# Weight sums moved from the mixer into the attention, and one chunk of convolution taps moved to ScalarE and GpSimd

## Chip, cores and metric

The kernel runs on one core of a Trainium2 chip. The metric is device time in microseconds (us) of one execution. Engines in the profile: PE is TensorE (PEld its weight loads), DVE VectorE, ACT ScalarE, POOL GpSimd, SP the engine that issues most transfers.

## What is computed

Linear attention over 8 batches x 8 heads x 576 positions, a gated mixer with a causal convolution of 5 taps, and an FFT mixing step with layer norm and an MLP (512 to 2048 to 512).

```
phi(x): p = x @ w_phi; p -= max|p|; [exp(p), exp(-p)]
kv, z = phi(k)^T v, sum phi(k);   attn = phi(q) kv / (phi(q) z)
gate = sigmoid(sum_k conv_w[k] * x[s - 4 + k]);  x = (gate * (x @ w_val)) @ w_out
u = x + real(fft(fft(x, axis=seq), axis=feature))
un = layernorm(u);  out = u + relu(un @ w_ch1) @ w_ch2
```

The weights are 64-bit floats in memory; the kernel converts them itself. The MLP's matrix products use a scheme with 7 products of 2x2 blocks in place of 8, which needs sums of the four quarters of each weight block.

## The kernel before

**Attention.** 16 units (a pair of batches, a pair of heads) of 5 groups of positions make 80 steps, written out in a fixed order in `run_attention`: in each step every engine gets its share of several groups (projection `pj`, maximum L260, subtraction L263, exponentials, `kv`, `nm`, transposes). Each engine works in the order in which its instructions were written, and so does the SP queue.

**Conversions.** Between them run 21 generators `convert` (L116), started one after another about three steps apart, each advanced at steps 0, 3, 4, 5, 6 and 8 after its start: load the raw words (L121), split low words on ScalarE (L131), three VectorE instructions on 128x1024 words (L133, L134, and the add at L135, which the profile shows as L62, the helper's line, `mt<-mt,cv`), exponent on ScalarE (L137), sign on ScalarE and two GpSimd multiplications (L139 to L141), then `done`. 16 of the 21 are blocks of `w_ch1` and `w_ch2` (`conv_mlp`, L376): their `done` stores four quarters, 512 KB, in `s_scr` in DRAM. Tile `mt` has two buffers, so L133 of a piece waits for the store of the piece two before it.

**Mixer.** The last steps of the attention and the mixer are noted as operations with costs and due times (`note_*`); `place_ops` (L1137) orders them per engine; operations that list two engines ("vp") go to VectorE or GpSimd as the planner sees fit, and its model lets GpSimd and VectorE operations on SBUF operands exclude each other. Per batch: taps of four channel chunks (`note_taps`: ScalarE the first, VectorE the other four of each), sigmoid, products `val` with w_val, gate, products `ps` with w_out, the FFT products. 16 times `note_sums` (L382) loads four quarters from `s_scr` to tile `ws`, makes four sums on GpSimd and stores them. The layer norm of the first block (`ln_first`) is put in by `ln0`, so many steps after each batch (L1093). For the first batch, taps of chunk 0 are made in the attention's last four steps (`tap_steps`, L484).

**MLP.** `note_mlp` runs 5 blocks of positions; its weights come from `s_scr` (`note_weights`, L681), and are split in two parts each.

Of the kernel before, what the change touches and what calls it, by code (L numbers as in the profile page):

```python
# [30 lines left out]
def f32(ap):  # L31
    return ap.bitcast(F32)
# [33 lines left out]
def attention_moe_mixer_kernel(  # L66
# [48 lines left out]

    def convert(i, src, n, shape, halve, done):  # L116
        raw = P["xf"].tile([128, 1024, 2], I32, tag="xf", name="raw64")[:, 0:n]
# [22 lines left out]
        nc.gpsimd.tensor_tensor(out=w, in0=w, in1=f32(ex), op=ALU.mult)  # L140
        nc.gpsimd.tensor_tensor(out=w, in0=w, in1=sg, op=ALU.mult)  # L141
        yield
        done(w.rearrange("p (k f) -> p k f", k=shape[0]))
# [60 lines left out]
    stg = pool(early, "stg", 2, side=R)  # L204
    vraw_p = pool(early, "vraw", 2, side=R)
    ps_pj = pool(early, "ps_pj", 2, PSUM, side=R)
    ap1 = pool(att, "ap1", 1)
# [165 lines left out]
    def slices(i, j, q):  # L373
        return s_scr[i][j // (i + 1)][q, :, j % (i + 1)].rearrange("q p o f -> p q (o f)")

    def conv_mlp(n, j, i):  # L376
        def done(t):
            nc.sync.dma_start(out=slices(i, j, slice(0, 4)), in_=t.rearrange("p (q o) f -> p q (o f)", o=2))
        s = (w_ch1, w_ch2)[i][j].bitcast(I32).rearrange("o p (q f) -> o p q f", q=4)
        return convert(n, s, 1024, (8,), False, done)  # L380

    def note_sums(n):  # L382
        i, j = wsteps[n]
        t = later("ws")
        a21, a11, a12, a22 = (t[:, k] for k in range(4))
        k21, k11, k12, k22 = keys = [("ws", k) for k in range(4)]
        o_dma([(t, slices(i, j, slice(0, 4)))], [], keys, 512)
        o_tt("p", a22, a21, a22, ALU.add, 256, [k21, k22], [k22])
        o_tt("p", a21, a11, a21, ALU.subtract, 256, [k11, k21], [k21])
        o_tt("p", a11, a22, a11, ALU.subtract, 256, [k22, k11], [k11])  # L390
        o_tt("p", a12, a12, a11, ALU.subtract, 256, [k12, k11], [k12])
        o_dma([(slices(i, j, slice(4, 8)), t)], keys, [("s", i, j)], 512)

# [5 lines left out]
    def put_table(dst, src):  # L399
        r, n = src.shape  # L400
        t = stg.tile([128, 580], F32, tag="tab", name="tab")
        nc.sync.dma_start(out=t[0:r, 0:n], in_=src)
        yield
        hi_act(dst, t[0:r, 0:n])
        yield
# [13 lines left out]
    def open_mix():  # L419
        p = pool(gx, "g0", 1, side=R)  # L420
        ws = pool(vx, "ws", 1, side=R)
        psv = pool(vx, "psv", 1, PSUM, side=R)
# [4 lines left out]
        for i in range(2):  # L427
            late["pv", i] = psv.tile([128, NE + 2], F32, name=f"val{i}")
            late["gv", i] = P["g"].tile([128, NE], F32, tag="gv", name="gv")
            late["gs", i] = P["g"].tile([128, 2, NE], F32, tag="gs", name="gs")  # L430
        late["ws"] = ws.tile([128, 4, 256], F32, name="ws")
        late["pa"] = psa.tile([128, 2, 512], F32, name="acc")
# [30 lines left out]

    wsteps = [(i, j) for j in range(NJ) for i in range(2)]

    def load_x(b):
# [17 lines left out]
    def tap_steps():  # L484
        t, acc = late["xf", 0], late["sg", 0]
        act.activation(out=acc, in_=shifted(t, 0, 4), func=ACTF.Copy, scale=cw[:, 0, 4:5])
        for k in range(4):
            vec.scalar_tensor_tensor(
                out=acc, in0=shifted(t, 0, k), scalar=cw[:, 0, k:k + 1], in1=acc, op0=ALU.mult, op1=ALU.add
            )  # L490
            yield

# [11 lines left out]
    def note_taps(b, m):  # L504
# [3 lines left out]
        acc, k = (s, sk) if first else (later("pa")[:, :, 0:HS], "pa")  # L508
        if b or m:
            o_act(acc, shifted(t, m, 4), ACTF.Copy, 685, [xk], [k], scale=cw[:, m, 4:5])  # L510
# [170 lines left out]
    def note_weights(c, n, first=[]):  # L681
# [11 lines left out]
        src = s_scr[c][j][q].rearrange("p n k f -> p (n k f)")  # L693
        o_dma([(f32(l), src)], [("s", c, x) for x in ((j,), (2 * j, 2 * j + 1))[c] if q > 3] + first + (over(s) if c == 0 and n < RING[0] else []), [lk], (128, 256)[c])
        o_hi(h, f32(l), cols, [lk], [hk])
# [253 lines left out]
    def note_W(b, c):  # L949
# [4 lines left out]
        for a in range(2):  # L954
# [10 lines left out]
            if c == 2 and a == 0:  # L965
                r = later(("xr", b % 2))
                o_hi(r[0:1], p[0:1], NE, [k], [("xr", b % 2, 0)])
                o_lo("v", r[32:33], p[0:1], r[0:1], NE, [k, ("xr", b % 2, 0)], [("xr", b % 2, 1)])
            o_act(t[:, c, a], p, ACTF.Copy, NE, [k] + [("s",) + wsteps[-1]] * w, [("x2", w, c, a)])
        if c >= 2:  # L970
# [86 lines left out]
    def note_mix():  # L1057
        rings = [[(("ps", i), later(("ps", i))) for i in range(n)] for n in (4, 5)]
        nonlocal ring
        ring = cycle(rings[0])  # L1060
        sums = iter(range(len(wsteps)))
        SUMS = [(1, 0, 1, 0, 1)] * 5 + [(1, 0, 0, 0, 0), (0,) * 5]

        def add_sums(n):
            for i in range(n):
                k = next(sums, None)
                if k is not None:
                    in_place(note_sums, k)

        ln0 = chain(ln_first(0), ln_first(1))  # L1070
# [6 lines left out]
        for b in range(NB - 1):  # L1077
            note_x(b + 1)
            for i, c in enumerate((0, 2, 1, 3)):
                if i < 3:  # L1080
                    note_taps(b + 1, i)
                    note_V(b + 1, i)
                note_W(b, c)
                add_sums(SUMS[b][i])
            add_sums(SUMS[b][4])
            note_taps(b + 1, 3)
# [5 lines left out]
            note_SD(b)  # L1092
            for k in range((0, 2, 1, 2, 1, 0, 0)[b]):  # L1093
                in_place(next, ln0, None)
# [434 lines left out]
```

## Time and profile before

| what | us |
|---|---|
| median of 3 runs | 1338.03 (1337.85 to 1338.59) |
| profiled execution | 1339.93 |
| its span, first to last instruction | 1338.1 |
| TensorE busy | 1302.2 (97%) |
| VectorE busy | 1186.8 (89%) |
| ScalarE busy | 925.5 (69%) |
| GpSimd busy | 699.2 (52%) |

Busy time is the time in which an engine executes something; matmuls are pipelined, so a busy TensorE isn't one at its peak. The attention takes the span's first 311 us, the mixer up to about 640 us, the MLP the rest. Idle time counts where the engine is the one that the others wait for, so the profile is read stage by stage.

### The profile page before, as it was taken

Reading aid. Unit: us, or ns where it says so; the run is one execution under the profiler, and the core shown is the slowest. Engines: PE = TensorE matmul, PEld = TensorE weight load, DVE = VectorE, ACT = ScalarE, POOL = GpSimd, SP = SyncE. Lnnn points to the kernel's source line nnn. Section 1 sums busy time; section 2 is a strip of 40 time slices with the busy share of each in tenths; the row PEclk is TensorE's granted clock in tenths of the full one; section 3 lists DMA queues with packets and bytes.
Section 4 is the critical chain, followed back from the end, with each engine's and each line's share of the span. In section 5 each row is a group of like instructions: output and inputs, shape, how many; then the busy total and the mean of one; then the engine's idle time right before and its main releaser. Section 6 shows DMA issues by size and latency. Waiting matters only on the chain.

```text
span 1338.1 us, 30770 instructions
## 1 busy us (share of the span) xinstructions
PE 1302.2 (97%) x11952; PEld 1188.0 (89%) x11952; DVE 1186.8 (89%) x1900; ACT 925.5 (69%) x1874; POOL 699.2 (52%) x599
## 2 busy tenths in 40 slices
PE   8999999999899998999999999999999999999998
PEld 7888888888899998998888888888888888889997
DVE  7999999989898998979998998898889989888875
ACT  6888888866555546565877686777777676776662
POOL 1534343404467566536655774488457945583321
PEclk9999999999999999999999999999999999999999
DMA  7578878643344453334633463347333743345322
GB/s 273 172 264 275 277 260 289 209 180 118 116 150 147 134 161 111 124 121 155 219 104 102 155 220 108 98 135 240 108 102 103 231 144 103 107 142 182 106 86 88
DMA packets 151598, 214.63 MB, mean 160 GB/s; under 512 B 16790, under 2 KB 112278, under 8 KB 151452
## 3 DMA queue, kind: packets, MB, share of 16 engines
q1 hardware_dynamic: 146992, 203.05, 47.5%
q10 hardware_dynamic: 4460, 9.62, 1.9%
q8 instruction: 94, 1.54, 0.5%
q14 instruction: 52, 0.43, 0.1%
HBM read 165.63 MB, written 46.99 MB: 159 GB/s over the span
## 4 chain that ended last, share of the span: by engine, by line
PE 74%; DVE 18%; DMA 2%; ACT 2%; issue 2%; POOL 1%; SPq 0%; DVEq 0%; POOLq 0%; ACTq 0%
PE x L62 15%; PE cx L62 15%; PE cy L62 11%; PE ps L62 10%; PE y L62 8%; PE val L62 4%; PE z L62 4%; DVE y L263 3%; DVE m L260 3%; DVE acc L62 2%; PE kv L62 2%; PE pj L62 2%; PE nm L62 2%; DVE mt L62 2%; PE yt L313 1%
## 5 line engine op out<-in xcount | busy, mean ns | idle before, releaser
L62 POOL TENSOR_TENSOR r<-r 128x256 fp32r<-128x256 f32 (+1 forms) x301 | 292.6, 989 | 242.8 <-ACT r L62 228.7
L62 PE MATMUL x<-un,r 128*128 128x462 f32 (+1 forms) x960 | 221.7, 372 | 2.2 <-ACT c L62 1.4
L62 ACT ACTIVATE r<-r 128x256 fp32r<-128x256 f32 (+1 forms) x420 | 193.2, 486 | 42.0 <-DMA r<-s_scr 40.7
L62 PE MATMUL cx<-h,r 128*128 128x462 f32 (+1 forms) x960 | 213.9, 371 | 1.1 <-DVE acc L62 1.1
L62 PEld LDWEIGHTS x<-un,r 128*128 128x128 f32 x960 | 180.3, 188 | 23.9 <-DVE c L62 1.9
L62 PEld LDWEIGHTS cx<-h,r 128*128 128x128 f32 x960 | 180.3, 188 | 22.1 <-DVE acc L62 1.9
L62 PE MATMUL cy<-h,r 128*128 128x462 f32 (+1 forms) x720 | 160.2, 371 | 0.0
L62 PEld LDWEIGHTS cy<-h,r 128*128 128x128 f32 x720 | 135.4, 188 | 15.3
L62 PE MATMUL val<-xh,wv 128*128 128x290 f32 x768 | 116.5, 300 | 9.2 <-DVE gv L62 4.5
L62 PEld LDWEIGHTS val<-xh,wv 128*128 128x128 f32 x768 | 106.6, 189 | 13.1 <-DVE gv L62 6.2
L62 PE MATMUL y<-un,r 128*128 128x462 f32 (+1 forms) x480 | 113.6, 371 | 0.0
L62 DVE SCALAR_TENSOR_TENSOR acc<-xf,cw,acc 128x576 f32<-128x576 f32 x128 | 105.0, 824 | 8.2 <-ACT acc L62 7.6
L62 PE MATMUL ps<-ge,wo 128*128 128x290 f32 x768 | 108.1, 297 | 2.2 <-DVE fs L62 1.4
L62 PEld LDWEIGHTS ps<-ge,wo 128*128 128x128 f32 x768 | 104.7, 189 | 3.2 <-DVE fs L62 1.6
L140 POOL TENSOR_TENSOR mt<-mt,cv 128x1024 f32<-128x1024 f32 (+1 forms) x21 | 47.5, 2263 | 105.8 <-ACT cv L137 101.6
L62 PEld LDWEIGHTS y<-un,r 128*128 128x128 f32 x480 | 90.2, 188 | 10.3
L62 DVE TENSOR_TENSOR acc<-cx,acc 128x924 f32<-128x924 f32 (+1 forms) x80 | 88.8, 1110 | 11.7 <-PE cx L62 9.7
L260 DVE TENSOR_REDUCE m<-pj 128x8 f32<-128x1024 f32 (+1 forms) x80 | 88.6, 1108 | 9.3 <-PE pj L62 9.3
L62 PE MATMUL kv<-vraw,ke 128*64 128x66 f32 x2560 | 93.4, 225 | 1.2 <-DVE kvT L305 0.5
L62 PE MATMUL pj<-wp,kqraw 64*128 64x128 f32 x1152 | 87.9, 290 | 5.0 <-DMA kqraw<-in_k_dram 4.7
L62 PEld LDWEIGHTS kv<-vraw,ke 128*64 128x64 f32 x2560 | 81.7, 137 | 11.7 <-ACT ke L272 1.1
L62 ACT ACTIVATE h<-z 128x462 fp32r<-128x462 f32 (+1 forms) x120 | 66.4, 553 | 34.9 <-DVE z L62 31.1
(176 smaller groups left out, 2809.5 us busy)
## 6 DMA issues: line engine op xcount, KB each, us to landing
r<-s_scr SPq DMA_DIRECT2D x280, 128.0 KB, 2.2
r<-s_scr SPq DMA_DIRECT2D x140, 256.0 KB, 2.6
raw<-in_w_ch_dram SPq DMA_DIRECT2D x32, 512.0 KB, 5.9
vraw<-in_v_dram SPq DMA_DIRECT2D x16, 660.0 KB, 9.3
x_scr<-xT SPq DMA_DIRECT2D x32, 288.0 KB, 2.3
xf<-x_scr SPq DMA_DIRECT2D x8, 1152.0 KB, 6.5
u_scr<-u ACTq DMA_DIRECT2D x8, 1152.0 KB, 4.5
kqraw<-in_k_dram SPq DMA_DIRECT2D x15, 576.0 KB, 5.6
```

Source lines behind the costliest of these rows:

```text
L62: return lambda *a, **k: f(*(resolve(x) for x in a), **{n: resolve(x) for n, x in k.items()})
L140: nc.gpsimd.tensor_tensor(out=w, in0=w, in1=f32(ex), op=ALU.mult)
L260: nc.vector.tensor_reduce(out=m, in_=pv, axis=AX.X, op=ALU.max, apply_absolute_value=True)
L263: nc.vector.tensor_tensor(out=y, in0=pv, in1=m.unsqueeze(3).to_broadcast([128, 2, 2 * n, F]), op=ALU.subtract)
L313: nc.tensor.transpose(t[:, h, j, :], y[:, h, n + j, :], ident)
```

## The change

- `convert` gets a hook `also`, called right after the two GpSimd multiplications. For the 16 MLP pieces it makes the four sums on GpSimd from the quarters that are still in SBUF, into a tile `s` (pool `sums`, one buffer). `done` then makes two stores on the SP queue, of the quarters and of the sums.
- `note_sums` with its 16 loads, 64 sums and 16 stores in the mixer is gone, with tile `ws`, and the waits for the sums in `note_weights` and `note_W`.
- The tables are loaded through the same one-buffer pool (before: two buffers of `stg`).
- `tap_steps` also makes the taps of chunk 1 of the first batch: in each of four steps a scaled copy on ScalarE and an addition on GpSimd, after one more copy at the start. `note_taps(0, 1)` then only notes the sigmoid.
- The steps of `ln0` are spread (1, 1, 2, 1, 1, 0, 0) in place of (0, 2, 1, 2, 1, 0, 0).

```diff
--- before.py
+++ after.py
@@ -113,7 +113,7 @@
         mm(o, al, bh, start=False, stop=last)
 
 
-    def convert(i, src, n, shape, halve, done):
+    def convert(i, src, n, shape, halve, done, also=None):
         raw = P["xf"].tile([128, 1024, 2], I32, tag="xf", name="raw64")[:, 0:n]
         raw_k = raw.rearrange("p n t -> p (n t)").rearrange("p (k f) -> p k f", k=shape[0])
         if shape[0] == 8:
@@ -139,6 +139,8 @@
         nc.scalar.activation(out=sg, in_=hi32, func=ACTF.Sign)
         nc.gpsimd.tensor_tensor(out=w, in0=w, in1=f32(ex), op=ALU.mult)
         nc.gpsimd.tensor_tensor(out=w, in0=w, in1=sg, op=ALU.mult)
+        if also:
+            also(w.rearrange("p (k f) -> p k f", k=4))
         yield
         done(w.rearrange("p (k f) -> p k f", k=shape[0]))
         yield
@@ -203,6 +205,7 @@
     y_p = pool(early, "y", 2, side=R)
     stg = pool(early, "stg", 2, side=R)
     vraw_p = pool(early, "vraw", 2, side=R)
+    sums_p = pool(early, "sums", 1, side=R)
     ps_pj = pool(early, "ps_pj", 2, PSUM, side=R)
     ap1 = pool(att, "ap1", 1)
     qe_p = pool(att, "qe", 4)
@@ -374,22 +377,22 @@
         return s_scr[i][j // (i + 1)][q, :, j % (i + 1)].rearrange("q p o f -> p q (o f)")
 
     def conv_mlp(n, j, i):
-        def done(t):
-            nc.sync.dma_start(out=slices(i, j, slice(0, 4)), in_=t.rearrange("p (q o) f -> p q (o f)", o=2))
-        s = (w_ch1, w_ch2)[i][j].bitcast(I32).rearrange("o p (q f) -> o p q f", q=4)
-        return convert(n, s, 1024, (8,), False, done)
-
-    def note_sums(n):
-        i, j = wsteps[n]
-        t = later("ws")
-        a21, a11, a12, a22 = (t[:, k] for k in range(4))
-        k21, k11, k12, k22 = keys = [("ws", k) for k in range(4)]
-        o_dma([(t, slices(i, j, slice(0, 4)))], [], keys, 512)
-        o_tt("p", a22, a21, a22, ALU.add, 256, [k21, k22], [k22])
-        o_tt("p", a21, a11, a21, ALU.subtract, 256, [k11, k21], [k21])
-        o_tt("p", a11, a22, a11, ALU.subtract, 256, [k22, k11], [k11])
-        o_tt("p", a12, a12, a11, ALU.subtract, 256, [k12, k11], [k12])
-        o_dma([(slices(i, j, slice(4, 8)), t)], keys, [("s", i, j)], 512)
+        t = {}
+
+        def sums(w):
+            t["w"], t["s"] = w, sums_p.tile([128, 4, 256], F32, tag="s", name="s")
+            a21, a11, a12, a22 = (w[:, k] for k in range(4))
+            s21, s11, s12, s22 = (t["s"][:, k] for k in range(4))
+            nc.gpsimd.tensor_tensor(out=s22, in0=a21, in1=a22, op=ALU.add)
+            nc.gpsimd.tensor_tensor(out=s21, in0=a11, in1=a21, op=ALU.subtract)
+            nc.gpsimd.tensor_tensor(out=s11, in0=s22, in1=a11, op=ALU.subtract)
+            nc.gpsimd.tensor_tensor(out=s12, in0=a12, in1=s11, op=ALU.subtract)
+
+        def done(_):
+            for q, x in enumerate((t["w"], t["s"])):
+                nc.sync.dma_start(out=slices(i, j, slice(4 * q, 4 * q + 4)), in_=x)
+        src = (w_ch1, w_ch2)[i][j].bitcast(I32).rearrange("o p (q f) -> o p q f", q=4)
+        return convert(n, src, 1024, (8,), False, done, sums)
 
     def conv_taps(i):
         def done(t):
@@ -398,7 +401,7 @@
 
     def put_table(dst, src):
         r, n = src.shape
-        t = stg.tile([128, 580], F32, tag="tab", name="tab")
+        t = sums_p.tile([128, 580], F32, tag="tab", name="tab")
         nc.sync.dma_start(out=t[0:r, 0:n], in_=src)
         yield
         hi_act(dst, t[0:r, 0:n])
@@ -418,7 +421,6 @@
 
     def open_mix():
         p = pool(gx, "g0", 1, side=R)
-        ws = pool(vx, "ws", 1, side=R)
         psv = pool(vx, "psv", 1, PSUM, side=R)
         psa = pool(vx, "psa", 1, PSUM, side=R)
         for g, q in enumerate((p, P["g1"])):
@@ -428,7 +430,6 @@
             late["pv", i] = psv.tile([128, NE + 2], F32, name=f"val{i}")
             late["gv", i] = P["g"].tile([128, NE], F32, tag="gv", name="gv")
             late["gs", i] = P["g"].tile([128, 2, NE], F32, tag="gs", name="gs")
-        late["ws"] = ws.tile([128, 4, 256], F32, name="ws")
         late["pa"] = psa.tile([128, 2, 512], F32, name="acc")
 
     def open_mix2():
@@ -461,8 +462,6 @@
             late["ps", i] = ps.tile([128, 512], F32, name=f"ps{i}")
         open_mlp()
 
-    wsteps = [(i, j) for j in range(NJ) for i in range(2)]
-
     def load_x(b):
         t = P["xf"].tile([128, 4, S + 4], F32, tag="xf", name="xf")
         late["xf", b] = t
@@ -483,11 +482,15 @@
 
     def tap_steps():
         t, acc = late["xf", 0], late["sg", 0]
-        act.activation(out=acc, in_=shifted(t, 0, 4), func=ACTF.Copy, scale=cw[:, 0, 4:5])
+        for m in range(2):
+            act.activation(out=late["sg", m], in_=shifted(t, m, 4), func=ACTF.Copy, scale=cw[:, m, 4:5])
         for k in range(4):
             vec.scalar_tensor_tensor(
                 out=acc, in0=shifted(t, 0, k), scalar=cw[:, 0, k:k + 1], in1=acc, op0=ALU.mult, op1=ALU.add
             )
+            p = P["g"].tile([128, 2, NE], F32, tag="gs", name="tap")[:, :, 0:HS]
+            act.activation(out=p, in_=shifted(t, 1, k), func=ACTF.Copy, scale=cw[:, 1, k:k + 1])
+            gps.tensor_tensor(out=late["sg", 1], in0=late["sg", 1], in1=p, op=ALU.add)
             yield
 
     def note_x(b):
@@ -506,7 +509,7 @@
         xk, sk = ("xf", b % 2), ("sg", m % 2)
         first = b == 0 and m < 2
         acc, k = (s, sk) if first else (later("pa")[:, :, 0:HS], "pa")
-        if b or m:
+        if b or m > 1:
             o_act(acc, shifted(t, m, 4), ACTF.Copy, 685, [xk], [k], scale=cw[:, m, 4:5])
             for i in range(4):
                 op("v", S, lambda e, i=i: vec.scalar_tensor_tensor(
@@ -691,7 +694,7 @@
         h, l = (w[:, k].rearrange(("p k f -> p (k f)", "p n k f -> p (n k f)")[c]) for k in range(2))
         q = SLOT[ORDER[c][i]]
         src = s_scr[c][j][q].rearrange("p n k f -> p (n k f)")
-        o_dma([(f32(l), src)], [("s", c, x) for x in ((j,), (2 * j, 2 * j + 1))[c] if q > 3] + first + (over(s) if c == 0 and n < RING[0] else []), [lk], (128, 256)[c])
+        o_dma([(f32(l), src)], first + (over(s) if c == 0 and n < RING[0] else []), [lk], (128, 256)[c])
         o_hi(h, f32(l), cols, [lk], [hk])
         o_lo(K["w"], l, f32(l), h, cols, [lk, hk], [lk])
 
@@ -966,7 +969,7 @@
                 r = later(("xr", b % 2))
                 o_hi(r[0:1], p[0:1], NE, [k], [("xr", b % 2, 0)])
                 o_lo("v", r[32:33], p[0:1], r[0:1], NE, [k, ("xr", b % 2, 0)], [("xr", b % 2, 1)])
-            o_act(t[:, c, a], p, ACTF.Copy, NE, [k] + [("s",) + wsteps[-1]] * w, [("x2", w, c, a)])
+            o_act(t[:, c, a], p, ACTF.Copy, NE, [k], [("x2", w, c, a)])
         if c >= 2:
             c0 = c - 2
             fk = [("fs", 0), ("fs", 1)]
@@ -1058,15 +1061,6 @@
         rings = [[(("ps", i), later(("ps", i))) for i in range(n)] for n in (4, 5)]
         nonlocal ring
         ring = cycle(rings[0])
-        sums = iter(range(len(wsteps)))
-        SUMS = [(1, 0, 1, 0, 1)] * 5 + [(1, 0, 0, 0, 0), (0,) * 5]
-
-        def add_sums(n):
-            for i in range(n):
-                k = next(sums, None)
-                if k is not None:
-                    in_place(note_sums, k)
-
         ln0 = chain(ln_first(0), ln_first(1))
         tail = note_tail()
         next(tail)
@@ -1081,8 +1075,6 @@
                     note_taps(b + 1, i)
                     note_V(b + 1, i)
                 note_W(b, c)
-                add_sums(SUMS[b][i])
-            add_sums(SUMS[b][4])
             note_taps(b + 1, 3)
             note_V(b + 1, 3)
             if b == NB - 2:
@@ -1090,7 +1082,7 @@
                 break
             note_FD(b)
             note_SD(b)
-            for k in range((0, 2, 1, 2, 1, 0, 0)[b]):
+            for k in range((1, 1, 2, 1, 1, 0, 0)[b]):
                 in_place(next, ln0, None)
         drain(ln0)
         b = NB - 2
```

## Rows read from the trace of the kernel before

**Rows 1.** The page, engine line: busy time, share of the span, instructions.
```profile
PE 1302.2 (97%) x11952; PEld 1188.0 (89%) x11952; DVE 1186.8 (89%) x1900; ACT 925.5 (69%) x1874; POOL 699.2 (52%) x599
```

**Rows 2.** Busy time by stage: stretch, its length, engines, clock, DMA share, GB/s.
```profile
65.00:265.00 200.00, 193.74 (x4155) 172.90 (x4156) 187.79 (x328) 168.82 (x318) 76.32 (x35) 1.00 0.79 266
265.00:311.00 46.00, 44.84 (x990) 40.14 (x986) 38.32 (x73) 30.67 (x69) 8.07 (x5) 1.00 0.40 143
311.00:530.00 219.00, 206.15 (x1603) 199.50 (x1603) 201.01 (x380) 122.93 (x238) 126.48 (x120) 0.99 0.42 138
...
640.00:1338.00 698.00, 692.25 (x3302) 620.33 (x3301) 609.20 (x873) 485.42 (x1005) 403.34 (x378) 1.00 0.45 136
```

**Rows 3.** Chain of waits, 140 to 175 us: start, length, instruction.
```profile
145.33 1.47 DVE mt L133
...
150.55 1.15 PE nm L62 x32
```

**Rows 4.** Timeline, GpSimd and VectorE at the end of one conversion: start, length.
```profile
167.42 2.37 POOL L141 TENSOR_TENSOR mt<-mt,cv 128x1024 f32<-128x1024 f32 x1 [1.95 <-ACT cv L139]
...
169.83 0.68 DVE L133 TENSOR_SCALAR mt<-raw 128x1024 int32<-128x1024 int32 x1
170.43 0.69 DVE L134 TENSOR_SCALAR cv<-raw 128x1024 int32<-128x1024 int32 x1
171.03 1.22 DVE L62 SCALAR_TENSOR_TENSOR mt<-mt,cv 128x1024 f32<-128x1024 f32 x1
```

**Rows 5.** Instructions on tile `mt`: ns min/median/max, first and last start.
```profile
L133 DVE TENSOR_SCALAR mt<-raw x21: 164/685/1827, 16.3 to 255.9; 128x1024 int32<-128x1024 int32 x20, 128x20 int32<-128x20 int32 x1
```

**Rows 6.** Instructions on tile `ws`, the sums: same columns.
```profile
L62 POOL TENSOR_TENSOR ws<-ws x64: 727/737/1614, 311.4 to 558.0; 128x256 f32<-128x256 f32 x64
```

**Rows 7.** Timeline, 549.9 to 553.2 us: VectorE and GpSimd on SBUF operands.
```profile
550.51 3.47 DVE L62 TENSOR_TENSOR A<-A,s 128x924 f32<-128x924 f32 x2
551.55 3.03 POOL L62 TENSOR_TENSOR ws<-ws 128x256 f32<-128x256 f32 x2
```

**Rows 8.** DMA, 65 to 265 us, us to landing; and one stretch by engine.
```profile
s_scr<-mt SPq DMA_DIRECT2D x15, 512.0 KB, 8.7
...
182.00:191.00 9.00, 8.76 (x202) 7.87 (x201) 8.86 (x16) 7.87 (x16) 3.21 (x3) 1.00 1.04 372
```

**Rows 9.** Timeline of the first part of the mix; in brackets idle time before.
```profile
312.17 5.72 DVE L62 SCALAR_TENSOR_TENSOR acc<-xf,cw,acc 128x576 f32<-128x576 f32 x7 [0.85 <-ACT acc L62]
...
318.31 1.87 PE L62 MATMUL val<-xh,wv 128*128 128x290 f32 x12 [1.27 <-DVE gv L62]
...
339.06 3.17 POOL L62 TENSOR_TENSOR ws<-ws 128x256 f32<-128x256 f32 x4 [4.15 <-DMA ws<-s_scr]
...
348.69 2.77 POOL L62 TENSOR_TENSOR ws<-ws 128x256 f32<-128x256 f32 x3 [6.47 <-DMA ws<-s_scr]
...
352.87 0.40 ACT L62 ACTIVATE xr<-ps 1x290 fp32r<-1x290 f32 x1 [4.54 <-POOL xr L453]
...
354.63 1.90 PE L62 MATMUL val<-xh,wv 128*128 128x290 f32 x12 [2.06 <-DVE gv L62]
```

**Rows 10.** Groups, 311 to 560 us: busy, mean ns, idle before and its ender.
```profile
L62 POOL TENSOR_TENSOR ws<-ws 128x256 f32<-128x256 f32 x64 | 52.4, 818 | 36.1 <-DMA ws<-s_scr 31.5 <-DVE xs L342 1.9
L62 POOL TENSOR_TENSOR xh<-xf,xh 128x576 fp32r<-128x576 f32 x16 | 25.0, 1577 | 7.6 <-ACT xh L62 6.4 <-ACT c L62 1.2
...
L62 ACT ACTIVATE acc<-xf,cw 128x576 f32<-128x576 f32 x30 | 22.3, 746 | 0.6
...
L62 DVE TENSOR_TENSOR ge<-gs,ge 128x580 fp32r<-128x580 f32 x13 | 11.6, 890 | 0.0
L62 DVE TENSOR_TENSOR xh<-xf,xh 128x576 fp32r<-128x576 f32 x12 | 11.2, 938 | 0.0
```

**Rows 11.** TensorE's timeline, then a stretch with the granted clock, near 527 us.
```profile
526.55 1.97 PE L62 MATMUL val<-xh,wv 128*128 128x290 f32 x9 [1.84 <-DVE gs L62]
...
528.00:530.00 2.00, 2.00 (x11) 2.00 (x10) 1.97 (x3) 1.06 (x2) 2.00 (x2) 0.50 0.69 254
```

## The prediction

> **What bounds the kernel now.** First the page's engine line and one table of busy time by stage: TensorE has 97% of the span [rows 1], but its idle time is uneven [rows 2]. From 640 us to the end (the MLP, 698 us) it is busy 692.25 us, so nothing in the change, which touches no instruction there, can gain there. In the stretch of the mix from 311 to 530 us it is busy 206.15 of 219 us: 12.85 us idle, VectorE at 201.01. In the attention (65 to 265 us, where the weights are converted) VectorE is busy 187.79 of 200 us, GpSimd only 76.32, the DMA engines 0.79 at 266 GB/s. There the kernel has two bounds that take turns: in the chain of waits, at a step that holds a conversion, VectorE's L133 lies on the chain, and a step later it is TensorE's `nm` [rows 3]. I counted the chain's pieces: for 13 of the 16 conversions of `w_ch` one of VectorE's conversion instructions is on it.
>
> So GpSimd's free half in the attention looks like the place for the sums. What matters is when they run there, hence next the neighbours of L141, GpSimd's last instruction of a conversion. It ends at 169.79 us (167.42 + 2.37); VectorE starts L133 of the next piece at 169.83, then L134 and the add, 2.4 us in one block to 172.25 [rows 4]. I measured this distance for all 15 pieces that have a successor: in 13 of them L133 starts between 1.3 us before and 0.8 us after the end of L141, in two 3.7 and 4.6 us after it. The new sums start exactly at the end of L141.
>
> **The sums in the attention (costs).** They add 16 x 4 GpSimd operations of 128x256, median 0.737 us [rows 6], so 2.95 us in a piece's cycle of 12.0 us (L133: 21 times, first at 16.3, last at 255.9, 239.6 / 20 [rows 5]). GpSimd has the time: 76.32 + some 47 us of 200. But L133 and GpSimd exclude each other: alone it takes 0.685 us, behind a running L141 up to 1.827 [rows 5]; at 145.33 it took 1.47 on the chain because L141 was running [rows 3]. L134 is the same operation in the same shape. The third, an add of two SBUF operands, has no meeting with GpSimd in this trace; the nearest row is that of two VectorE operations on two SBUF operands against two sums, which took turns: 3.47 us for the two, 3.03 for the two sums instead of 1.47 [rows 7]. So I take it that all three wait and that turns alternate. Each piece then costs VectorE the rest of the running sum (0 to 0.74) plus a whole sum before L134 and one before the add: 1.5 to 2.2, taken 1.7, since L133 mostly arrives half a microsecond into the first sum (0.24 + 2 x 0.74 = 1.7). 13 pieces: 22.1 us. VectorE can take up part: it idles 12.2 of 200 us, 0.73 a piece, much of it in steps where TensorE leads; I take 0.5 off, 13 x 1.2 = **+15.6 us**. From below: only L133 waits, half a sum, and that is taken up: 0. From above: 13 x 2.2 = 28.6.
>
> GpSimd spans can be read in two ways. Four sums that nothing disturbed took 3.17 us together [rows 9], 0.79 each by spacing against 0.737 by the span. The Trainium skill, Perfetto Trace Analysis, section GPSIMD Engine Instruction, says to time GpSimd by start-to-start spacing and not by its spans; by that rule a collision costs 0.1 us more and the sum above some 1.4 us more, and the row agrees with the rule. I stay with the span and leave the difference to the range.
>
> **Stores and buffers.** In the attention a second 512 KB store follows each of 16 pieces: 8.4 MB in 200 us, 42 GB/s on top of 266. The DMA engines have carried 372 GB/s over 9 us at full share [rows 8]; 0.79 x 308 / 266 = 0.91, so it fits, with later landings. On the SP queue the second store waits for the sums; behind it are queued the loads of the next pieces, `x_scr` stores and the next unit's q, k, v, which the queue mostly reaches ahead of need. The tables' single buffer is loaded and read steps apart: 0. The sums' tile has one buffer: sums 2.95 (5.4 when interleaved with 2.4 of VectorE) + landing 8.7 [rows 8] = 11.7 to 14.1 us against the cycle of 12.0. If it is late, the sums of the next piece start later and miss the conversion, which ends the lateness: self-limiting. I cost it at 0 (bounds -3, by collisions missed, to +5).
>
> **The taps in the last steps.** Four GpSimd adds of 128x576 (the nearest row takes 1.58 us [rows 10]) and five ScalarE copies (0.75) come into 265 to 311 us, where GpSimd is busy 8.07 and VectorE 38.32 of 46 us [rows 2]: cover enough, apart from collisions with the four VectorE taps there (two SBUF operands): **+0.5** (0 to 4 x 0.7 = 2.8).
>
> **What the mix gains.** (a) Four VectorE taps of channel chunk 1 go: seven take 5.72 us, 3.3 for four, at the start of the mix; behind them `gv` waits and TensorE idles 1.27 us for it [rows 9]. VectorE is the bound there: -3.0 (0 to -3.3). (b) At 352.87 ScalarE has waited 4.54 us for a GpSimd memset that stands behind three sums, and TensorE then idles 2.06 us [rows 9]. Without the sums: -2.0. (c) GpSimd gets back 52.4 us of sums (64 x 0.818) and 31.5 us of waiting for their loads [rows 10]. The planner can give it remainders that VectorE now takes, 25 of `ge` and `xh`, 22.8 us together [rows 10]. At 1.55 us each it may take a third: some 7 us off VectorE, of which a third shows: -2.5. (d) At 526.55 TensorE waits 1.84 us for VectorE in a layer norm step, and its granted clock is 0.50 in the stretch from 528 to 530 us, after those gaps [rows 11]. The layer norm's steps also move, one earlier into the first batch; half of some 3 us: -1.5. Sum **-9.0** (0 to -15, which is all idle time there and the slow clock). The removed loads and stores are not on the chain: 0.
>
> **Sum.** +15.6 + 0.5 - 9.0 = +7.1. The profiled execution took 1339.93 us (span 1338.1), 1.9 above the median of 1338.03; the difference is put on the median: 1345.
>
> **The rivals.** *It is faster*: the collisions don't cost what I think. TensorE is busy 193.74 of 200 us in the attention; if it is the bound there, a late VectorE costs only what its idle time doesn't cover; likewise if the sums' buffer comes free 3 us late each time and they run behind the conversion. Then +3 in place of +15.6: 1338 + 3 + 0.5 - 9 = 1332. It decides at 0.7 us a collision (13 x 0.7 = 9.1, the gain in the mix): below, the kernel is faster. Against it speaks the chain through L133. The Trainium skill, Perfetto Trace Analysis, section Identifying the Most-Contended Engine, calls matmul busy time a bad measure and weight-load time a good one; by weight loads TensorE has 172.90 of 200 us [rows 2], so VectorE leads, and the chain agrees; by matmul busy time this rival would be the forecast. *A draw*: half the collisions, or a gain of 13 in the mix: 1338 + 8.6 + 0.5 - 9 = 1338. *Heavier*: late landings also reach the `mt` buffers (L133 waits for the store of two pieces before: 1 us at six pieces) and VectorE takes up nothing: 22.1 + 6 + 0.5 - 9 = +19.6, 1358.
>
> **Chances.** Forecast 0.46, faster 0.28, draw 0.17, heavier 0.09. Three runs of before lie 0.74 us apart; 0.2% (2.7 us) is what can be told from no change. Faster 0.28, same 0.17, slower 0.55. The range, 1330 to 1357, leaves out the ends of the first and the last case. The forecast's own is 1341 to 1352.
>
> **What would show it.** Right: in the attention the medians of L133, L134 and the add rise from 0.69, 0.69 and 1.22 to about 1.0, 1.4 and 1.9, and the last conversion comes 13 to 18 us later; `gv` starts some 2 us sooner after the attention's end; no memset wait; the MLP's 698 us unchanged. Wrong: those durations are as before, or they rise and the last conversion is not later (then TensorE leads), or GpSimd's sums wait for a landing.

## The result, and the profile after

| | median, us | range | runs |
|---|---|---|---|
| before | 1337.94 | 1335.9 to 1338.59 | 4 |
| after | 1347.95 | 1347.41 to 1348.65 | 4 |

The ratio is 1.0078, with an interval of 1.006 to 1.0095: the changed kernel is slower by 10 us, where +7 was forecast (1345). The profiled execution of after took 1347.41 us with a span of 1345.6, 7.5 us above the span of before.

The engine line of after's page, which answers to [rows 1]:

```profile
PE 1302.1 (97%) x11952; PEld 1190.1 (88%) x11952; DVE 1193.3 (89%) x1895; ACT 925.5 (69%) x1878; POOL 721.7 (54%) x604
```

Nothing of the loss is visible there: TensorE is busy for as long as before, and VectorE only 6.5 us longer. The table by stage (stretch, its length, busy time of PE, PEld, DVE, ACT, POOL, clock, DMA share, GB/s) shows more. Its stretches answer to those of [rows 2], moved by what the stages before them grew:

```profile
66.00:282.00 216.00, 195.79 (x4183) 174.19 (x4182) 204.00 (x332) 170.10 (x322) 142.08 (x96) 1.00 0.83 283
282.00:327.00 45.00, 43.30 (x960) 39.04 (x960) 38.23 (x69) 32.32 (x69) 15.51 (x13) 1.00 0.42 153
327.00:545.00 218.00, 211.69 (x1666) 207.17 (x1665) 203.84 (x394) 124.99 (x255) 81.08 (x63) 0.99 0.22 74
645.00:1345.60 700.60, 694.70 (x3314) 622.67 (x3313) 609.05 (x874) 488.64 (x1010) 406.72 (x381) 1.00 0.46 136
```

In the attention VectorE is now busy 204.00 of 216 us, and TensorE idles 20 us where it idled 6. In the mix TensorE has 6.3 us of idle time left of 12.85. The MLP is as it was.

Four distances between the same instructions add up to the whole difference. The first conversion starts at 17.9 us (before 16.3): +1.6. From its L133 to that of the last conversion 253.8 us (239.6): +14.2. From there to the first `val` product 57.1 us (56.6): +0.5. From there to the end of the last computing instruction 1013.3 us (1022.1): -8.8. The sum is +7.5. Each number is one profiled execution, and such numbers scatter: a second trace of the same kernel (e11 below) has +0.2, +15.9, +0.5 and -7.7. So the +1.6 at the start is not the change's, and the attention and the mix are known to one or two us.

Instructions on the tiles `mt`, `cv` and `s` (ns min/median/max, first and last start), to be read against [rows 5, 6]:

```profile
L133 DVE TENSOR_SCALAR mt<-raw x21: 167/819/1842, 17.9 to 271.7; 128x1024 int32<-128x1024 int32 x20, 128x20 int32<-128x20 int32 x1
L134 DVE TENSOR_SCALAR cv<-raw x21: 170/1233/1252, 18.5 to 272.3; 128x1024 int32<-128x1024 int32 x20, 128x20 int32<-128x20 int32 x1
L62 DVE SCALAR_TENSOR_TENSOR mt<-mt,cv x21: 180/1748/1766, 19.1 to 272.9; 128x1024 f32<-128x1024 f32 x20, 128x20 f32<-128x20 f32 x1
...
L386 POOL TENSOR_TENSOR s<-mt x16: 734/913/1705, 86.7 to 283.5; 128x256 f32<-128x256 f32 x16
L387 POOL TENSOR_TENSOR s<-mt x16: 726/1186/1203, 87.4 to 284.2; 128x256 f32<-128x256 f32 x16
L388 POOL TENSOR_TENSOR s<-s,mt x16: 727/1184/1723, 88.1 to 284.9; 128x256 f32<-128x256 f32 x16
```

One such meeting on the timeline of after (start, length; idle time in brackets), which answers to [rows 4]:

```profile
177.29 2.38 POOL L141 TENSOR_TENSOR mt<-mt,cv 128x1024 f32<-128x1024 f32 x1 [3.26 <-ACT cv L139]
179.74 1.23 POOL L386 TENSOR_TENSOR s<-mt 128x256 f32<-128x256 f32 x1
180.94 1.19 POOL L387 TENSOR_TENSOR s<-mt 128x256 f32<-128x256 f32 x1
182.08 1.72 POOL L388 TENSOR_TENSOR s<-s,mt 128x256 f32<-128x256 f32 x1
183.88 0.73 POOL L389 TENSOR_TENSOR s<-mt,s 128x256 f32<-128x256 f32 x1
...
179.69 0.68 DVE L133 TENSOR_SCALAR mt<-raw 128x1024 int32<-128x1024 int32 x1
180.29 1.24 DVE L134 TENSOR_SCALAR cv<-raw 128x1024 int32<-128x1024 int32 x1
181.45 1.76 DVE L62 SCALAR_TENSOR_TENSOR mt<-mt,cv 128x1024 f32<-128x1024 f32 x1
```

The two engines take turns: L133, a sum, L134, a sum, the add, a sum. VectorE's block lasts 3.44 us (179.69 to the next instruction at 183.13), alone 2.34. Over the 15 conversions that have a predecessor with sums (or would have had), the blocks exceed 2.33 us by 18.2 us in all; in before the same sum is 3.1. This number is called the surplus below. It grew by 15.2 us, and the attention by 14.2 (in e11's trace by 16.4 and 15.9).

### The profile page after: what moved, and what is told of

The parts are those of the page before. It is cut to its first block, busy times and chain, and to the rows that moved or that the text cites. A ratio compares the mean times of both kernels' runs of the same rounds, so it can differ in the third digit from the quotient of the medians.

```text
span 1345.6 us, 30779 instructions
## 1 busy us (share of the span) xinstructions
PE 1302.1 (97%) x11952; PEld 1190.1 (88%) x11952; DVE 1193.3 (89%) x1895; ACT 925.5 (69%) x1878; POOL 721.7 (54%) x604
## 4 chain that ended last, share of the span: by engine, by line
PE 74%; DVE 18%; ACT 3%; issue 2%; DMA 2%; SPq 0%; DVEq 0%; ACTq 0%
PE cx L62 14%; PE x L62 14%; PE ps L62 12%; PE cy L62 11%; PE y L62 7%; PE val L62 5%; PE z L62 4%; DVE y L266 3%; DVE m L263 3%; DVE mt L62 2%; DVE acc L62 2%; PE kv L62 2%; PE pj L62 2%; PE nm L62 2%; DVE mt L133 1%
## 5 line engine op out<-in xcount | busy, mean ns | idle before, releaser
L62 POOL TENSOR_TENSOR r<-r 128x256 fp32r<-128x256 f32 (+1 forms) x308 | 301.5, 997 | 243.6 <-ACT r L62 214.5
L263 DVE TENSOR_REDUCE m<-pj 128x8 f32<-128x1024 f32 (+1 forms) x80 | 88.7, 1108 | 10.6 <-PE pj L62 10.6
L62 PE MATMUL nm<-kvT,qe 128*64 128x65 f32 x2304 | 82.5, 222 | 15.8 <-DVE xs L345 15.1
L62 PEld LDWEIGHTS kv<-vraw,ke 128*64 128x64 f32 x2560 | 82.4, 138 | 16.4 <-DVE kvT L308 2.9
```

Of the source, the lines that this page charges most:

```text
L62: return lambda *a, **k: f(*(resolve(x) for x in a), **{n: resolve(x) for n, x in k.items()})
L263: nc.vector.tensor_reduce(out=m, in_=pv, axis=AX.X, op=ALU.max, apply_absolute_value=True)
```

## The experiments

Every kernel was timed beside before on the same chip. e1 to e4 shared one chip, the other eight another.

| kernel | median, us | before beside it | ratio | interval |
|---|---|---|---|---|
| e2 before + sums in the attention | 1354.21 | 1339.76 | 1.011 | 1.0089 to 1.013 |
| e1 after without sums | 1338.22 | 1339.76 | 0.9984 | 0.9971 to 0.9997 |
| e8 after, sums in halves | 1340.74 | 1341.27 | 1.0002 | 0.9992 to 1.0012 |
| e4 after, sums held back | 1335.62 | 1339.76 | 0.9977 | 0.9963 to 0.999 |
| e3 before + early taps | 1337.53 | 1339.76 | 0.9985 | 0.9976 to 0.9995 |
| e5 before + new `ln0` spread | 1335.72 | 1341.27 | 0.9962 | 0.995 to 0.9974 |
| e9 e4 with the old spread | 1342.04 | 1341.27 | 1.0016 | 1.0004 to 1.0028 |
| e7 after without early taps | 1344.40 | 1341.27 | 1.0032 | 1.002 to 1.0044 |
| e11 after again | 1348.94 | 1340.40 | 1.0064 | 1.005 to 1.0078 |
| e12 after, `xh` on VectorE | 1345.16 | 1340.40 | 1.0034 | 1.0022 to 1.0046 |
| e10 e4 without early taps | 1336.17 | 1340.40 | 0.9962 | 0.9948 to 0.9976 |
| e13 e4, `xh` on VectorE | 1334.92 | 1340.40 | 0.9951 | 0.9937 to 0.9966 |

### Is it the turns, or the transfers?

**e2_sums_only** is before with the sums made where after makes them, but not stored; the mixer goes on making its own.

```diff
+        if also:
+            also(w.rearrange("p (k f) -> p k f", k=4))
...
+        def sums(w):
+            t = sums_p.tile([128, 4, 256], F32, tag="s", name="s")
...
-        return convert(n, s, 1024, (8,), False, done)
+        return convert(n, s, 1024, (8,), False, done, sums)
```

> The kernel before plus the 64 sums at their new place in the attention, not stored; the mixer still makes its own. Theory: L134 rises to 1.23 us and the add to 1.75, the conversions end 14 us later than before, nothing is gained in the mix: 1338 + 14.5 = 1352 us. Rival (transfers): 1338 us, and unchanged durations. A third, that sums only cost because their tile waits for its store: no store here, so 1338 to 1340.

```profile
L133 DVE TENSOR_SCALAR mt<-raw x21: 166/740/1824, 16.9 to 270.3; 128x1024 int32<-128x1024 int32 x20, 128x20 int32<-128x20 int32 x1
L62 DVE SCALAR_TENSOR_TENSOR mt<-mt,cv x21: 178/1750/1766, 18.1 to 271.5; 128x1024 f32<-128x1024 f32 x20, 128x20 f32<-128x20 f32 x1
```

(Tile `mt`, as above.) The surplus is 18.3 us and the distance from the first to the last L133 is 253.4 us, as in after, with no added transfer and no store for the sums' buffer to wait for. The sums alone cost the attention 14 us, as expected.

**e1_no_sums** is after without the four sums: both stores are kept, the second one stores the quarters again.

```diff
-            t["w"], t["s"] = w, sums_p.tile([128, 4, 256], F32, tag="s", name="s")
...
+            t["w"] = t["s"] = w
```

> The changed kernel without its 64 sums: the second store writes the quarters once more, so the transfers and the SP queue are those of the change and the output lacks the sums. Theory (shared port: VectorE's conversion instructions and the sums take turns): L133, L134 and the add fall back to 0.69, 0.69 and 1.22 us, the conversions end about 15 us sooner, and the gain of the mix is left: 1338 - 9 + 1 = 1330 us. Rival (the second stores and the fuller queue cost the time): conversions end as late as in the changed kernel, 1345 to 1348 us.

The surplus is 3.3 us, so with the sums the turns go too, and 11 to 13 us of after with them (0.9984 of before, where after has 1.0064 and 1.0078). But 1330 was not reached. The attention's 242.9 us are 3.3 more than in before, with both stores on the queue and no turns; and the part from the first `val` to the end gains 7.1 us. The 3.3 us are what I had costed at 0 (bounds -3 to +5). What of them is the transfers and what is scatter isn't settled. The distance was 239.0 to 240.2 us in the three kernels without second stores and without turns (before, e3, e5) and 242.0 to 246.3 in the five with second stores (e1 and the kernels of e4's kind), so some of it is likely the stores; beside the turns they show little (253.4 in e2 without them, 253.8 to 255.5 with them in after, e7, e11 and e12).

**e8_halves** is after with each sum as two GpSimd instructions of 128x128.

```diff
+            for o, x, y, f in (
+                (s22, a21, a22, ALU.add), (s21, a11, a21, ALU.subtract),
+                (s11, s22, a11, ALU.subtract), (s12, a12, s11, ALU.subtract),
+            ):
+                for h in (slice(0, 128), slice(128, 256)):
+                    nc.gpsimd.tensor_tensor(out=o[:, h], in0=x[:, h], in1=y[:, h], op=f)
```

> After, with each of the four sums made as two halves of 128x128, so eight GpSimd instructions with the same result. Theory: VectorE's three instructions each wait for no more than the GpSimd instruction that is running, so the price of a collision goes with the length of one turn, not with the work that is queued. Turns of half the length: the surplus of VectorE's three instructions falls from 18.2 us over 15 pieces to about 9 to 10 (above half, as a halved GpSimd instruction will take over half of 0.737 us), and the kernel takes 1339 to 1341 us. Rival: the price goes with GpSimd's whole work beside the conversion; it is the same or larger: surplus 18 us or more and 1348 us or more.

```profile
L134 DVE TENSOR_SCALAR cv<-raw x21: 168/949/968, 18.0 to 265.4; 128x1024 int32<-128x1024 int32 x20, 128x20 int32<-128x20 int32 x1
L62 DVE SCALAR_TENSOR_TENSOR mt<-mt,cv x21: 180/1480/1486, 18.6 to 266.0; 128x1024 f32<-128x1024 f32 x20, 128x20 f32<-128x20 f32 x1
...
L391 POOL TENSOR_TENSOR s<-mt,s x32: 442/460/1436, 90.5 to 279.5; 128x128 f32<-128x128 f32 x32
```

(Tiles `cv`, `mt`, `s`.) GpSimd has more work than in after (8 x 0.46 = 3.7 us a piece against 2.95), and yet the surplus falls to 10.6 us and the kernel takes 1340.74, as the theory has it. So the price goes with the length of one turn and not with the work that is queued. A turn of 0.737 us lengthens L134 by 0.55 (0.685 to 1.233) and the add by 0.53; a turn of 0.46 us lengthens each by 0.26. Each time that is the GpSimd instruction less 0.2 us.

**e4_gate1** holds the sums of a piece back until the next piece's three VectorE instructions are done: GpSimd first copies one column of their result, and the sums follow.

```diff
+        if held:
+            nc.gpsimd.tensor_copy(out=gate, in_=w[:, 0:1])
+            held.pop(0)()
         yield
         nc.scalar.activation(out=sg, in_=hi32, func=ACTF.Sign)
...
-            also(w.rearrange("p (k f) -> p k f", k=4))
+            held.append(lambda: also(w.rearrange("p (k f) -> p k f", k=4)))
```

> The changed kernel with the sums of a piece held back until VectorE has finished the next piece's three instructions (a GpSimd copy of one column of the next piece's tile, then the sums, then the next multiplications); stores follow. Same work, same transfers. Theory: collisions gone, L134 and the add at 0.69 and 1.22 us, conversions end within 3 us of those of the kernel before, the mix keeps its gain: 1330 to 1333 us. Rival (GpSimd's longer chain is the cost, not the port): L140 and L141 come later and hold up the pieces, 1340 to 1348 us.

```profile
162.04 0.19 POOL L139 COPY gate<-mt 128x1 f32<-128x1 f32 x1 [3.85 <-DVE mt L62]
162.18 0.74 POOL L391 TENSOR_TENSOR s<-mt 128x256 f32<-128x256 f32 x1
162.88 0.74 POOL L392 TENSOR_TENSOR s<-mt 128x256 f32<-128x256 f32 x1
163.58 0.74 POOL L393 TENSOR_TENSOR s<-s,mt 128x256 f32<-128x256 f32 x1
164.40 0.74 POOL L394 TENSOR_TENSOR s<-mt,s 128x256 f32<-128x256 f32 x1
...
162.24 1.21 DVE L270 TENSOR_REDUCE m<-pj 128x8 f32<-128x1024 f32 x1
```

(Timelines of GpSimd and VectorE.) The sums now lie beside VectorE instructions that read PSUM (`kvT`, and `m`, which takes its 1.21 us as in before), each of the four sums has a median of 0.74 us, L134 and the add are at 0.686 and 1.215 again, and the surplus is 3.4 us. The same GpSimd work in the same stretch costs nothing in turns: where it stands decided, not how much it is. The kernel takes 1335.62 us beside a before of 1339.76, 4.1 less; 5 to 8 less was expected of it (1330 to 1333 beside 1338), and the rival is out.

### Where does the mix's gain come from?

**e3_taps_only** is before with the early taps alone (the lines of the change in `tap_steps` and `note_taps`).

> The kernel before plus only the taps of chunk 1 on ScalarE and GpSimd in the attention's last four steps. Prediction's step: +0.5 us in those steps, -3.0 at the start of the mix: 1335.5 us. Rival (VectorE's first stretch of the mix is not the bound, or the planner reorders to its loss): 1338.

It gains 2.2 us, as expected; but the parts say something else. From the first `val` to the 384th it takes 108.1 us, longer than before's 106.3. The gain comes after that, and no run tells why: the expected number was met, but not where it was expected.

**e5_ln0_only** is before with one line changed.

```diff
-            for k in range((0, 2, 1, 2, 1, 0, 0)[b]):
+            for k in range((1, 1, 2, 1, 1, 0, 0)[b]):
```

> Before, with the steps of the first layer norm spread (1, 1, 2, 1, 1, 0, 0) instead of (0, 2, 1, 2, 1, 0, 0) and nothing else. The prediction's term (d) put 1.5 us of gain on these steps and on the clock behind the wait at 526.55 us. Theory: this shows without the sums' removal, 1336.5 us where before takes 1338 (span from the first val to the last 272.7 us against 274.2). Rival: the wait at 526.55 goes only because GpSimd is freed of the sums, so the new spread alone gives nothing: 1338, and val to val 274.

Both expectations fall: it gains 5.5 us, the most of any single edit. The stretch from 520 to 540 us, which holds the wait of [rows 11], and the 20 us ahead of it, in e5 and then in before (columns as in the table by stage):

```profile
500.00:520.00 20.00, 19.85 (x148) 19.57 (x147) 18.67 (x35) 10.79 (x21) 10.24 (x10) 1.00 0.23 80
520.00:540.00 20.00, 20.00 (x153) 19.83 (x153) 18.55 (x35) 12.54 (x30) 13.78 (x13) 1.00 0.40 139
```

```profile
500.00:520.00 20.00, 17.54 (x124) 16.48 (x123) 17.54 (x30) 9.59 (x18) 8.98 (x10) 1.00 0.42 138
520.00:540.00 20.00, 18.16 (x127) 17.69 (x126) 17.75 (x35) 12.62 (x29) 17.00 (x14) 0.91 0.17 54
```

In e5 TensorE is busy for all but 0.15 us of this and its clock stays at 1.00. In before the waits begin at 513 us, and the clock loses 0.09 x 20 = 1.8 us besides. Over 480 to 580 us the idle time falls by 3.8 us (TensorE busy 98.72 against 94.88), which with the 1.8 of the clock is about the whole gain. From first to last `val` e5 takes 268.3 us against 274.2.

**e9_gate_oldln0** is e4 with that line as in before.

> The kernel that holds the sums back behind the next piece's conversion, with the layer norm's steps spread as before, (0, 2, 1, 2, 1, 0, 0). Theory (term (d)): 1.5 us slower than with the new spread, 1337 where that took 1335.6 and before takes about 1339. Rival: the spread is worth nothing once GpSimd is free in the mix, 1335.6.

1.0016 where e4, on the other chip, had 0.9977, a difference of 5 us where 1.5 or none was expected: the spread is worth as much without the sums in the mix as with them.

**e7_after_oldtaps** is after with the taps of chunk 1 back on VectorE at the start of the mix, and **e11_after_again** is after itself, on the same chip.

> After, with the taps of channel chunk 1 put back on VectorE at the start of the mix. Theory (term (a), -3.0 in the mix, and +0.5 at the end of the attention): 2.5 us slower than after, 1350.5 where after takes 1348; TensorE again waits over 1 us for gv early in the mix. Taps alone on before gave 2 us. Rival: with GpSimd free of the sums the planner makes up for the four taps elsewhere, and the kernel stays at 1348.

> After itself, unchanged, as the comparison for the three others on the same chip. The first result was 1.0078 of before; a chip on which before takes 1340 us should give 1349 to 1351. If it comes nearer to 1.0032, then the 4 us between after and after with the old taps were a difference of chips and not of kernels.

After without the early taps is faster, by 4.5 us (1344.40 against 1348.94); both expectations of e7 had it the same or slower. That e11 has 1.0064, nearer to the 1.0078 of the first result than to e7's 1.0032, says that the difference is one of kernels and not of chips. So the early taps, worth 2 us on before, cost 4.5 us in after. `xh` holds a batch's x in two parts, a rounded one that ScalarE makes and a remainder that VectorE or GpSimd makes, in four chunks of channels; the `val` products read both. Timelines in after, and the stretch by engine there:

```profile
350.21 0.44 PE L1323 MATMUL xt<-ident,xs 128*128 128x128 f32 x2 [1.64 <-ACT xT L62]
350.40 0.78 PE L62 MATMUL val<-xh,wv 128*128 128x290 f32 x4
353.17 3.13 PE L62 MATMUL val<-xh,wv 128*128 128x290 f32 x16 [1.99 <-DVE xh L62]
...
348.35 4.15 POOL L62 TENSOR_TENSOR xh<-xf,xh 128x576 fp32r<-128x576 f32 x3 [21.61 <-ACT xh L62]
...
352.14 0.98 DVE L62 TENSOR_TENSOR xh<-xf,xh 128x576 fp32r<-128x576 f32 x1
...
348.80:358.80 10.00, 6.60 (x36) 6.37 (x37) 9.32 (x18) 4.09 (x9) 5.87 (x9) 0.83 0.16 61
```

and the same place in e7:

```profile
350.56 0.93 PE L62 MATMUL val<-xh,wv 128*128 128x290 f32 x5 [1.02 <-DVE xh L62]
...
348.24 1.65 POOL L62 TENSOR_TENSOR xh<-xf,xh 128x576 fp32r<-128x576 f32 x1 [0.61 <-ACT xh L62]
...
348.90 1.60 DVE L62 TENSOR_TENSOR xh<-xf,xh 128x576 fp32r<-128x576 f32 x1
351.94 0.75 DVE L62 TENSOR_TENSOR xh<-xf,xh 128x576 fp32r<-128x576 f32 x1
...
348.40:358.40 10.00, 8.39 (x64) 7.87 (x60) 9.93 (x21) 4.20 (x9) 3.65 (x7) 1.00 0.16 61
```

In after the wait for `gv` of [rows 9] is gone, and TensorE runs on to the next things that are late: `xT` (a copy by ScalarE, which has just made four parts of `xh`) and the `xh` of the second batch. The planner gives GpSimd three of the four remainders there (4.15 us) and not one, but it is not GpSimd that TensorE waits for: those three are done at 352.50, and the wait ends with the one that VectorE begins only at 352.14, behind taps. The last remainder is no later than in e7 (24.3 us after the first `val` in both), but in e7 the one that TensorE waits for at this place is done after 22.1 us (350.50). The early waits are gathered into two of 1.64 and 1.99 us that stand together, and behind them the granted clock is 0.83 over ten us, against 1.00 in e7: with levels of 1.2 and 2.4 GHz that is 3.4 us at the lower one, which cost 1.7 us of work. Waits 4.3 against 3.0 us, and the clock 1.7: that makes 3.0 us, and the first 384 `val` starts are 2.8 us further apart (104.2 against 101.4).

**e12_after_xh_v** takes the choice from the planner for that batch.

```diff
-                o_lo("vp", l, x, h, S, [("xf", b % 2), ("xh", c, 0)], [("xh", c, 1)])
+                o_lo("v" if b == 1 else "vp", l, x, h, S, [("xf", b % 2), ("xh", c, 0)], [("xh", c, 1)])
```

> After, with the remainders xh of the second batch only on VectorE (0.75 us each) and not, as the planner then chose, three of four on GpSimd (1.4 us each). Theory: TensorE's waits near 350 us (1.64 for xT, 1.99 for xh) and the granted clock of 0.83 there come from xh being late; on VectorE the last xh comes some 1.5 us sooner, the clock stays at 1.00 and the kernel gains 2 to 4 us against after: 1345 where after takes 1348. Rival: VectorE leads in this stretch, its later work (acc, gs) comes later by as much, and nothing is gained: 1348.

```profile
349.86 1.26 PE L62 MATMUL val<-xh,wv 128*128 128x290 f32 x5 [1.39 <-DVE xh L62]
...
349.06 0.75 DVE L62 TENSOR_TENSOR xh<-xf,xh 128x576 fp32r<-128x576 f32 x1
...
351.19 1.42 DVE L62 TENSOR_TENSOR xh<-xf,xh 128x576 fp32r<-128x576 f32 x2
...
348.80:358.80 10.00, 8.44 (x58) 7.77 (x59) 8.96 (x20) 4.44 (x10) 4.78 (x8) 1.00 0.16 60
```

One wait of 1.39 us is left of the two, the clock stays at 1.00, the first 384 `val` take 100.9 us, and the kernel gains 3.8 us on after: in the time and the clock the theory holds, and the edit gives back most of what the early taps had cost. The last remainder, though, is done only 0.5 us sooner after the first `val` (23.8 us against 24.3) and not 1.5; what comes sooner is the end of TensorE's wait for them, 21.0 us after the first `val` in place of 24.3. The planner also orders the work around it anew, which no run tells apart from the edit.

### A better kernel

**e13_gate_xh_v** is e4 with the line of e12, **e10_gate_oldtaps** is e4 without the early taps.

> The sums held back behind the next piece's conversion, with early taps and new spread, and the remainders xh of the second batch only on VectorE. Theory: 2 to 4 us less than with the planner's choice, 0.9977 becomes 0.995 to 0.996. Rival: no gain, 0.9977.

> The sums held back behind the next piece's conversion, the new spread of the layer norm's steps, and the taps of channel chunk 1 put back on VectorE in the mix. Theory: once the layer norm's steps are spread, the early taps cost the mix time: they take TensorE past its wait for gv, it meets the wait for xh of the second batch sooner, and its clock falls there. So without them 3 to 4 us less than with them: 0.9977 becomes 0.995 (1333 us where before takes 1340). Rival: the taps gain 2 us here too, as they did on before: 0.999, 1339.

e13 has the lowest time of all, 0.9951 of before (5.5 us) and 14 us under after on the same chip. That is within its theory, but its interval overlaps that of e4, which ran on the other chip. e10 comes to 0.9962, between its theory (0.995) and e4's 0.9977, and not at the rival's 0.999; here too the intervals overlap, so a cost of the early taps is shown in after alone. And e5, one line on before, has 0.9962 as well; e10 is e5 with the sums in the attention, held back, and the tables' one-buffer pool, so there they are worth nothing that can be told from noise. With the early taps besides, but without the new spread, the kernel is even a little slower than before (e9, 1.0004 to 1.0028). That the sums in the attention are worth anything at all, held back or not, isn't shown. On this chip the attention of e13, e10 and e9 took 246.3, 245.5 and 243.9 us, in e4 on the other 242.0. Between 60 and 300 us TensorE of e13 has nine waits, 7.2 us in all and up to 1.5, for which the profile names no releaser (before: 0.5 us in all); what they are stays open.

## Why the prediction was right or wrong

The sign and the size were right (+10 by the medians, +7.5 by the spans, +7.1 forecast), but several terms were not, and their errors cancelled.

**The bound and the place of the sums: right.** Sums that start at the end of L141 meet the next conversion. 13 of the 15 blocks are longer than alone, L133, L134 and the add stand at 0.82, 1.23 and 1.75 us where 1.0, 1.4 and 1.9 were forecast, and the last conversion comes 15.8 us later, within the 13 to 18. e2 shows that the sums do it, e8 that turns do, e4 that the place does.

**The price of a meeting: two errors that cancel.** I took 1.7 us of waiting and 0.5 of it taken up by idle VectorE, 1.2 net. Measured: 15.2 / 13 = 1.17 us of waiting, of which the attention shows 14.2 / 13 = 1.09 (in e11's trace 16.4 us of waiting and 15.9 in the attention). A turn costs 0.55 us and not 0.74, and next to nothing is taken up: VectorE's 12 idle us in [rows 2] do not lie where the delay could use them. +15.6 was forecast, +14.2 and +15.9 measured. The measured price of a turn lies below the span of a sum, so reading GpSimd by spacing, which would have raised the forecast by 1.4, was further off than reading it by the span. The row that seemed to speak for spacing (sums 0.81 us apart) may hold a dependence as well: in e4 the sums start 0.70 us apart where the next one doesn't read the result of the one before, and 0.82 where it does (163.58 to 164.40), and in the mixer each sum reads or overwrites what the one before used. The Trainium skill, Perfetto Trace Analysis, section GPSIMD Engine Instruction, asks for that reading by spacing. The Trainium skill, SBUF — State Buffer, section Who interferes with whom, says that the second engine is blocked for the whole instruction of the first. Of 0.737 us the runs show 0.55 as delay. That the two engines, when both have full queues, alternate instruction by instruction is what the timeline above shows.

**Stores and buffers: about right.** The `s` buffer was late twice (GpSimd's timeline of after):

```profile
139.74 0.73 POOL L386 TENSOR_TENSOR s<-mt 128x256 f32<-128x256 f32 x1 [1.83 <-DMA s_scr<-s]
...
206.00 1.71 POOL L386 TENSOR_TENSOR s<-mt 128x256 f32<-128x256 f32 x1 [2.08 <-DMA s_scr<-s]
```

The second time the sums came too late to delay the conversion that had started at 204.70, whose block took 2.34 us: the lateness limits itself, as forecast. The first time it pushed them into one (141.59) that they would have missed, for 0.7 us. Together that is near the 0 of the forecast; of the transfers e1 leaves some 3 us open.

**The taps, (a) and +0.5: wrong.** The end of the attention grew by 0.5 us as forecast, and the wait for `gv` went. But a gain of 3.0 was claimed and a loss was measured, 4.5 us in after. The step that failed is "VectorE is the bound there: -3.0": it named no next thing that would be late. That was `xh` of the second batch: ScalarE starts on it 18.8 us after the first `val` in after, 18.5 in before and 18.0 in e7, so the early taps do not bring it forward. On before alone the two terms came out nearly right (-2.2 for -2.5), but that was luck: the start of the mix, where the gain was to be, grew by 1.8 us (e3).

**(b), the memset wait: right.** No ScalarE wait for GpSimd's memset is left, nor the 2.06 us of TensorE behind it; e5, which keeps the sums in the mix, still has 1.85 us at that place.

**(c), the remainders: wrong in mechanism, its size not isolated.** Groups of after from 327 to 575 us (busy, mean ns, idle before), against [rows 10]:

```profile
L62 POOL TENSOR_TENSOR xh<-xf,xh 128x576 fp32r<-128x576 f32 x17 | 26.3, 1568 | 33.0 <-ACT xh L62 23.6 <-issue 8.6 <-POOL f L62 0.9
...
L62 DVE TENSOR_TENSOR ge<-gs,ge 128x580 fp32r<-128x580 f32 x12 | 9.1, 755 | 0.1
L62 DVE TENSOR_TENSOR xh<-xf,xh 128x576 fp32r<-128x576 f32 x11 | 8.4, 781 | 0.1
```

A third of 25 was to leave VectorE; two did. VectorE still saves 5.3 us (22.8 to 17.5), as each remainder takes 0.76 to 0.78 us in place of 0.89 to 0.94: which fits turns that went with the sums, though no run isolates it. (b) and (c) together were costed at -4.5; e7 against e5, which differ by the sums' place, shows -6.6 from the first to the last `val`: 2.1 us more than forecast, and no run divides it between the two.

**(d), the layer norm's steps: mis-sized.** -1.5 was forecast, -5.5 measured (e5). I looked at one wait and halved it; the waits before it and the clock behind it went too.

So the mix's -9.0, measured -8.8, is a sum of other terms. Before, e5, e7 and after follow each other by one step each; from the first `val` to the end of the last computing instruction the steps are -5.1 for the spread, -6.8 for the sums that are gone, and +3.0 for the early taps (+4.5 by the medians). The MLP is nearly unchanged, as forecast: 694.7 us from the first `cx` product to that end, before 696.0.

## What to carry to other kernels

Idle time of GpSimd is worth only what it leaves of VectorE's work beside it: before work is moved to GpSimd, look at which VectorE instructions run in the 3 us after the place, and put it beside those that read PSUM, or cut it into shorter instructions. Where a wait of TensorE is removed, name the next thing that is late before booking the gain; waits that come to stand together can cost the clock as well. And an edit of one line among several (the spread of `ln0`) deserves its own kernel: here it held the largest gain, and the rest together lost.

## What was not expected of the hardware

GpSimd and VectorE, each with instructions waiting that touch SBUF operands, alternated one by one; a turn of 0.737 us delayed VectorE by 0.55, one of 0.46 by 0.26. And TensorE's clock fell after waits that stood together: with waits of 1.02 and 0.58 us near 350 us the granted clock stayed at 1.00 (e7), with 1.39 too (e12), and with 1.64 and 1.99 us and 1 us of work between them it was 0.83 over ten us (after, and again in e11), in e3 with the same two waits (1.65 and 1.98) at the same place of the mix 0.69. The waits that cost the clock are longer as well as closer together, and no run tells the two apart.
